# A DiT attention block: V with its features on the partitions, Wo applied before the attention weights, and the gate applied to V Wo

## The chip, the cores and the metric

The kernel runs on one core of one Trainium2 chip. A core has a matrix engine (TensorE, PE in the profile; its weight loads are listed apart as PEld), a vector engine (VectorE, DVE), an engine for activations and copies (ScalarE, ACT), a general engine (GpSimd, POOL) and a queue engine (SyncE, SP) that here only issues transfers. The engines run independently and wait for one another by semaphores. TensorE writes only to PSUM, which has 8 banks of 2 KB per partition; the other engines carry results from PSUM to SBUF, the working memory of 128 partitions. The metric is the device time of one execution in microseconds; lower is better.

## The reference

The inputs are x (2 batches of 256 tokens with 1152 features), a condition c per batch, and the weights wqkv, wo and w_mod, all in bfloat16. Cut to what matters:

```python
mod = (silu(c) @ w_mod).reshape(B, 6, 1, D)      # shift, scale, gate used
h = layernorm(x) * (1 + scale_a) + shift_a
q, k, v = split(h @ wqkv)                        # each (2, 256, 1152)
p = softmax(einsum('bqd,bkd->bqk', q, k) * D ** -0.5)
a = einsum('bqk,bkd->bqd', p, v) @ wo
return x + gate_a * a                            # one gate row per batch
```

The gate has one value for each batch and output feature; it is the same for all tokens of a batch. P V Wo can be multiplied in either order, (P V) Wo or P (V Wo), and since the gate scales output features it can be put on V Wo as well as on the result.

## The kernel before, in words

Names: P = 128 partitions, KT = 9 blocks of 128 features, TT = 4 token tiles of 128 (tiles 0 and 1 are batch 0, tiles 2 and 3 batch 1), CW = 384 columns, NCH = 3 such chunks, NQ = 2 token tiles in a batch, N = 256, T = 512 tokens.

The front of the program, up to the scores, is not touched. It loads x and the weights in one ordered list on the SP queue, normalises x, turns it so that features lie on the partitions (hT, 128 x 9 x 512), and forms K and Q with features on the partitions (qkT). The scores of a batch (s_ps) are a product of those two. The softmax goes over VectorE and ScalarE (scores, exps, probs, lines 590 to 612), and the weights P are turned by DMA (turn, line 614) into pT, with key tokens on the partitions. On the way VectorE accumulates the gate in 18 steps (gate_steps, gacc): each scales one 128-row block of the gate's weights and adds it. When they are done, two partition_all_reduce instructions on GpSimd (line 645), one for each batch, sum over partitions and leave the gate in gate_bc, in float32, the same row on every partition.

The part that the change rewrites has three stages on TensorE:

- V (v_group, line 622): for each token tile and 384-column chunk, nine matmuls with hT as the stationary operand and the V weights as the moving one, 108 in all. V comes out with tokens on the partitions; ScalarE casts each bank to v_sb (evac, first argument False).
- P V (line 663): for each batch and 128-feature block, two matmuls with v_sb stationary and pT moving, 36 in all of 256 columns. The result has features on the partitions; the casts to attnT alternate between VectorE and ScalarE.
- Wo (line 675): for each token tile, chunks of output columns of nine matmuls each, attnT stationary and wO moving. Tiles 0 to 2 have three chunks of 384, tile 3 has 448, 320, 256 and 128. VectorE multiplies each bank by the gate into ga, adds x into o_sb, and SP stores the rows. The last chunk goes another way: the 128 columns of wO for it are multiplied by the gate beforehand (gated_columns into wo_last, three times on VectorE between other work, once on GpSimd), an identity matmul brings x into the bank, and ScalarE copies it out and issues the store itself (line 711).

The order of the work is written by hand. Every instruction of TensorE, VectorE, ScalarE, SP and GpSimd is recorded through a wrapper (its line, 85, is what the profile shows for nearly all of them), and pin fixes each engine's order to that of the program text. PSUM banks are handed out in turn from a ring of eight (bank, line 66). A queue that waits for one instruction holds back everything behind it.

Of the kernel before, what the change touches and what calls it, by code (L numbers as in the profile page):

```python
# [8 lines left out]
ALU = mybir.AluOpType  # L9
AX = mybir.AxisListType  # L10
F32 = mybir.dt.float32
BF16 = mybir.dt.bfloat16
# [4 lines left out]
def kernel(  # L17
# [9 lines left out]
    nc = tc.nc  # L27
    P = 128
    B, N, D = x.shape
    T = B * N  # L30
    KT = D // P
    TT = T // P
    NQ = N // P
    CW = 384
    NCH = D // CW
# [10 lines left out]
    out_f = out.rearrange("b n d -> (b n) d")  # L46
# [7 lines left out]
    act = ctx.enter_context(tc.tile_pool(name="act", bufs=1))  # L54
    work = ctx.enter_context(tc.tile_pool(name="work", bufs=2))
    const = ctx.enter_context(tc.tile_pool(name="const", bufs=1))
# [9 lines left out]
    def bank(shape, name, dtype=None, where=None):  # L66
        if where is None:
            where = ring[turn_no[0] % len(ring)]
            turn_no[0] += 1
        return where[0].tile(shape, dtype or F32, tag=where[1], name=name)  # L70
# [21 lines left out]
    vec = _Rec(nc.vector, dve_seq)  # L92
    sca = _Rec(nc.scalar, act_seq)
    ten = _Rec(nc.tensor, pe_seq)
    spq = _Rec(nc.sync, sp_seq)
    gps = _Rec(nc.gpsimd, pool_seq)
# [13 lines left out]
    def one(t):  # L110
        return slice(t * P, (t + 1) * P)
# [3 lines left out]
    ident = const.tile([P, P], BF16)  # L115
    gps.memset(ident, 0.0)
    gps.affine_select(
        out=ident, in_=ident, compare_op=ALU.not_equal, fill=1.0, base=0,
# [8 lines left out]
        out=mask, in_=mask, compare_op=ALU.is_ge, fill=0.0, base=0,  # L127
# [3 lines left out]
        out=mask, in_=mask, compare_op=ALU.is_ge, fill=0.0, base=2,  # L131
# [4 lines left out]
    x_sb = act.tile([P, TT, D], BF16)  # L136
# [7 lines left out]
    chunks_w = [wpool.tile([P, KT, CW], BF16, tag=f"wchunk{i}", name="wV") for i in range(NCH)]  # L144
# [121 lines left out]
    hT = act.tile([P, KT, T], BF16)  # L266
# [69 lines left out]
    def evac(on_dve, out_ap, in_ap):  # L336
        if on_dve:
            return vec.tensor_copy(out=out_ap, in_=in_ap)
        return sca.copy(out=out_ap, in_=in_ap)
# [201 lines left out]
    wO = wmpool.tile([P, KT, D], BF16, tag="wH")  # L541
# [31 lines left out]
    for f in range(QACC, KT):  # L573
        ps = bank([P, T], "psQ")
# [6 lines left out]
    for b in range(B):  # L581
        s_ps = bank([P, NQ, N], "s_ps")
        for i in range(NQ):
            tq = b * NQ + i
            for k in range(KT):
                ten.matmul(s_ps[:, i, :], lhsT=qkT[:, k, tq * P : (tq + 1) * P], rhs=qkT[:, KT + k, tok(b)],
                           start=(k == 0), stop=(k == KT - 1))
        s_tiles.append(s_ps)

    nmxs, p_fs, rsums, pns, pT_sbs = {}, {}, {}, {}, []  # L590
# [26 lines left out]
            spq.dma_start_transpose(out=pT[:, :, i * P : (i + 1) * P], in_=pns[b][:, i, :])  # L617
        pT_sbs.append(pT)

    v_sb = act.tile([P, TT, D], BF16, tag="a1")  # L620

    def v_group(gidx):
        t, vc = divmod(gidx, NCH)
        wt = chunks_w[vc]
        ps = bank([P, CW], "ps")
        for k in range(KT):
            ten.matmul(ps, lhsT=hT[:, k, t * P : (t + 1) * P], rhs=wt[:, k, :], start=(k == 0), stop=(k == KT - 1))
        evac(False, v_sb[:, t, vc * CW : (vc + 1) * CW], ps)

    gate_bc = act.tile([P, B, D], F32, tag="gb")  # L630

    gate_steps(11)
# [12 lines left out]
        ar = gps.partition_all_reduce(gate_bc[:, b, :], gacc[:, b, :], P, bass.bass_isa.ReduceOp.add)  # L645
        tc.add_manual_dep(ar.ins, gate_done, SYNC_SCHED, reason="keep gpsimd off the shared port")

    for gidx in range(TT * NCH):
        v_group(gidx)

    attnT = act.tile([P, KT, T], BF16, tag="a2")
    TAIL = (128,)
    TAILW = sum(TAIL)
    wo_last = const.tile([P, KT, TAILW], BF16)

    def gated_columns(eng, k0, k1):
        eng.tensor_tensor(out=wo_last[:, k0:k1, :], in0=wO[:, k0:k1, D - TAILW :],
                          in1=gate_bc[:, B - 1, D - TAILW :].unsqueeze(1).to_broadcast([P, k1 - k0, TAILW]),
                          op=ALU.mult)

    gated_columns(gps, KT - 1, KT)

    for b in range(B):
        for gi, dv0 in enumerate(range(0, KT, 2)):
            ndv = min(2, KT - dv0)
            ps = bank([P, 2, N], "ps")
            for dd in range(ndv):
                dv = dv0 + dd
                for j in range(NQ):
                    ten.matmul(ps[:, dd, :], lhsT=v_sb[:, b * NQ + j, dv * P : (dv + 1) * P],  # L670
                               rhs=pT_sbs[b][:, j, :], start=(j == 0), stop=(j == NQ - 1))
            evac(gi % 2 == 0, attnT[:, dv0 : dv0 + ndv, b * N : (b + 1) * N], ps[:, :ndv, :])

    todo = {4: (0, 3), 6: (3, 6), 8: (6, KT - 1)}
    for t in range(TT):
        b = t // NQ
        o_sb = work.tile([P, D], BF16, tag="o_sb")
        if t < TT - 1:
            chunks = [(oc * CW, CW) for oc in range(NCH)]
            dma_after = {NCH - 1: (0, D)}  # L680
        else:
            chunks, c0 = [], 0
            for w_ in (448, 320, 256) + TAIL:
                chunks.append((c0, w_))
                c0 += w_
            dma_after = {1: (0, chunks[2][0]), 2: (chunks[2][0], D - TAILW), 3: (D - TAILW, D)}
        for ci, (c0, w_) in enumerate(chunks):
            cs = slice(c0, c0 + w_)
            last = (t == TT - 1) and (ci == len(chunks) - 1)
            pregated = (t == TT - 1) and c0 >= D - TAILW  # L690
            ps = bank([P, w_], "ps")
            if pregated:
                ten.matmul(ps, lhsT=ident, rhs=x_sb[:, t, cs], start=True, stop=False)
            for k in range(KT):
                ten.matmul(
                    ps, lhsT=attnT[:, k, t * P : (t + 1) * P],
                    rhs=(wo_last[:, k, c0 - (D - TAILW) : c0 - (D - TAILW) + w_] if pregated else wO[:, k, cs]),
                    start=(k == 0 and not pregated), stop=(k == KT - 1),
                )
            if pregated:  # L700
                sca.copy(out=o_sb[:, cs], in_=ps)
            else:
                ga = work.tile([P, 448], F32, tag="ga")
                vec.tensor_tensor(out=ga[:, :w_], in0=ps, in1=gate_bc[:, b, cs], op=ALU.mult)
                vec.tensor_tensor(out=o_sb[:, cs], in0=ga[:, :w_], in1=x_sb[:, t, cs], op=ALU.add)
                if t * NCH + ci in todo:
                    gated_columns(vec, *todo[t * NCH + ci])
            if ci in dma_after:
                d0, d1 = dma_after[ci]
                dma_eng = nc.scalar if last else spq  # L710
                dma_eng.dma_start(out=out_f[t * P : (t + 1) * P, d0:d1], in_=o_sb[:, d0:d1])

    pin(pe_seq)
    pin(dve_seq)
# [33 lines left out]
```

## Time and profile before

| | |
|---|---|
| Median of 3 runs | 95.46 us (95.27 to 95.66) |
| Profiled execution | 95.63 us, its span 93.9 us |
| PE busy | 89.2 us (95%), 664 matmuls |
| DVE busy | 69.6 us (74%) |
| ACT busy | 33.9 us (36%) |
| POOL busy | 20.8 us (22%) |
| First matmul of V | 51.67 us |
| First matmul of P V | 69.22 us |
| First matmul of Wo | 73.15 us |

The span is the time from the first to the last event that the profile of the execution shows; the execution's own time is a little longer. A line of the profile names the engine, the operation, its output and inputs as out<-in, the shapes, how often it ran, the busy time, and the idle time of its engine just ahead of it with what ended that. In the timeline the first two columns are the start and the length of a merged group, in microseconds; the last bracket is idle time and its releaser. In the windows each pair is busy time and number of pieces. The ends of matmuls are modelled, and spans on GpSimd are rough.

### The profile page before, as it was taken

The numbers are of one execution on the slowest core, as the hardware profiler recorded it, in microseconds if no ns is written. First come the engines' busy times: TensorE is split into PE (matmuls) and PEld (weight loads), VectorE is DVE, ScalarE is ACT, GpSimd is POOL, SyncE is SP. The second block draws the span as 40 slices with busy tenths as digits, with TensorE's granted clock in tenths as the row PEclk, the third lists the DMA queues.
The fourth block names the chain that finished last, engine by engine and source line by source line (L and its number), as shares of the span: only waits on it lengthen the run. The fifth ranks groups of instructions, "written<-read, shape, count | busy, mean of one in ns | idle before, by whom it ended". The sixth has DMA issues, their size and how long they took to land.

```text
span 93.9 us, 1692 instructions
## 1 busy us (share of the span) xinstructions
PE 89.2 (95%) x664; PEld 52.8 (56%) x664; DVE 69.6 (74%) x134; ACT 33.9 (36%) x69; POOL 20.8 (22%) x26
## 2 busy tenths in 40 slices
PE   3999999999999999999999999999999999999970
PEld 1348884545445444444478665656578665665660
DVE  2478789245997977999999899990028587888880
ACT  5188788002643600284220687324246200000010
POOL 5623000800000000000000000008999990002000
PEclk9999999999999999999999999999999999999999
DMA  2999999999999999999999702200000000312212
GB/s 23 345 282 374 372 397 362 369 410 407 407 405 410 414 408 412 402 373 365 381 407 410 296 17 56 63 0 0 0 0 0 0 0 8 125 42 83 114 45 92
DMA packets 17232, 21.31 MB, mean 227 GB/s; under 512 B 2249, under 2 KB 10569, under 8 KB 17225
## 3 DMA queue, kind: packets, MB, share of 16 engines
q1 hardware_dynamic: 16809, 21.17, 62.3%
q8 instruction: 5, 0.08, 0.3%
q10 hardware_dynamic: 416, 0.04, 0.3%
q14 instruction: 2, 0.02, 0.0%
HBM read 19.76 MB, written 1.18 MB: 223 GB/s over the span
## 4 chain that ended last, share of the span: by engine, by line
PE 91%; DVE 4%; issue 1%
PE ps L85 39%; PE psQ L85 19%; PE acc L85 11%; PE psK L85 7%; PE junk_ps L85 5%; PE s_ps L85 4%; PE tp L85 2%; PE psE L85 2%; PE psS L85 2%; DVE o_sb L85 2%; DVE ga L85 2%; PE psH L85 1%; DVE xc L85 1%; DVE junk L85 1%; PE bc_ps L85 0%
## 5 line engine op out<-in xcount | busy, mean ns | idle before, releaser
L85 POOL PARTITION_ALL_REDUCE gate_bc<-gacc x2 | 13.7, 6886 | 44.6 <-DVE gacc L85 44.6
L85 DVE SCALAR_TENSOR_TENSOR gacc<-wG,scT_f,gacc 128x1152 f32<-128x1152 bf16 x16 | 22.4, 1416 | 0.4
L85 PE MATMUL ps<-wV,hT 128*128 128x384 bf16 x108 | 17.7, 326 | 0.0
L85 PE MATMUL psQ<-hT,wQ 128*128 128x512 bf16 x81 | 17.6, 379 | 0.0
L85 PE MATMUL ps<-wO,attnT 128*128 128x384 bf16 (+3 forms) x108 | 17.2, 322 | 0.0
L85 PEld LDWEIGHTS <-attnT 128*128 128x128 bf16 x117 | 11.1, 98 | 6.5
L85 PEld LDWEIGHTS <-hT 128*128 128x128 bf16 x108 | 10.6, 98 | 6.9
L85 PEld LDWEIGHTS <-wK 128*128 128x128 bf16 x109 | 9.5, 97 | 6.9 <-issue 0.2
L85 PEld LDWEIGHTS <-wQ 128*128 128x128 bf16 x81 | 7.9, 98 | 9.6
L85 PE MATMUL acc<-hTs,wK 128*128 128x512 bf16 (+2 forms) x65 | 11.2, 314 | 0.0
L85 DVE TENSOR_TENSOR ga<-ps,gate_bc 128x384 f32<-128x384 f32 (+3 forms) x12 | 6.5, 545 | 3.0 <-PE ps L85 3.0
L85 ACT CAST qkT<-psQ 128x512 bf16<-128x512 f32 x9 | 4.9, 597 | 10.6 <-PE psQ L85 10.6
L85 DVE CAST attnT<-ps 128x512 bf16<-128x512 f32 (+1 forms) x6 | 3.5, 603 | 6.8 <-PE ps L85 6.8
L85 ACT CAST v_sb<-ps 128x384 bf16<-128x384 f32 x12 | 5.5, 476 | 7.9 <-PE ps L85 7.9
L85 PE MATMUL psK<-hTs,wK 128*128 128x512 bf16 x28 | 7.0, 379 | 0.0
L85 DVE TENSOR_TENSOR o_sb<-ga,x_sb 128x384 bf16<-128x384 f32 (+3 forms) x12 | 6.6, 548 | 0.4
L85 ACT CAST o_sb<-ps 128x128 bf16<-128x128 f32 x1 | 0.3, 265 | 17.3 <-PE ps L85 17.3
L85 PE MATMUL junk_ps<-junk 128*128 128x512 bf16 x11 | 4.9, 629 | 1.5 <-DVE junk L85 1.5
L85 DVE TENSOR_TENSOR hT<-hTs,held 128x512 bf16<-128x512 bf16 x9 | 5.8, 688 | 0.4 <-ACT held L85 0.4
L85 DVE BATCH_NORM_STATS2 stats<-x_sb 128x6 f32<-128x384 bf16 x6 | 3.1, 544 | 2.3 <-DMA x_sb<-in_x_dram 2.3
L85 PEld LDWEIGHTS <-junk 128*128 128x128 bf16 (+1 forms) x13 | 1.6, 134 | 5.0 <-issue 3.4
L85 PE MATMUL s_ps<-qkT 128*128 128x256 bf16 x36 | 4.1, 273 | 0.0
(81 smaller groups left out, 84.2 us busy)
## 6 DMA issues: line engine op xcount, KB each, us to landing
wG<-in_w_mod_dram SPq DMA_DIRECT2D x3, 864.0 KB, 12.5
wV<-in_wqkv_dram SPq DMA_DIRECT2D x3, 864.0 KB, 13.4
wO<-in_wo_dram SPq DMA_DIRECT2D x3, 864.0 KB, 9.0
wH<-in_w_mod_dram SPq DMA_DIRECT2D x2, 1152.0 KB, 9.3
wQ<-in_wqkv_dram SPq DMA_DIRECT2D x4, 576.0 KB, 11.7
wK<-in_wqkv_dram SPq DMA_DIRECT2D x7, 288.0 KB, 7.0
wS<-in_w_mod_dram SPq DMA_DIRECT2D x3, 320.0 KB, 6.3
x_sb<-in_x_dram SPq DMA_DIRECT2D x3, 288.0 KB, 3.4
```

What stands on the lines that cost most here:

```text
L85: r = fn(*a, **k)
```

## The change

V is formed with its features on the partitions, as Q and K already are: for each of nine feature blocks, nine matmuls with the V weights stationary and all 512 tokens moving, cast by ScalarE into vT. Then U = V Wo is formed for all tokens: vo(t, c0, w_) takes vT of one token tile as stationary and a chunk of wO as moving operand, and VectorE multiplies the bank by the batch's gate row into u_sb in bfloat16. Then attend(t, c0, w_) multiplies with P: pT stationary, u_sb moving, two matmuls for each token tile and chunk. VectorE adds x from SBUF and writes o_sb; for the last two chunks of tile 3 (on_act) an identity matmul brings x into the bank and ScalarE copies it out. The calls of vo and attend are interleaved in a written list. For batch 1 the last 384 columns are split into 256 and 128, and the last attend calls are split into a first and a last matmul step. o_sb now has all four token tiles. The columns of wO that were multiplied by the gate beforehand (wo_last, gated_columns) are gone, and so are v_sb, attnT and ga.

The stores are 288 KB each for tiles 0 and 1, then 192 KB of tile 3, 256 KB of tile 2, 64 KB of tile 3, 32 KB of tile 2, all on SP, and 32 KB of tile 3 on ScalarE's queue.

```diff
-    for gidx in range(TT * NCH):
-        v_group(gidx)
...
-    gated_columns(gps, KT - 1, KT)
...
+    vT = act.tile([P, KT, T], BF16, tag="a1")
+    for f in range(KT):
+        wt, i = chunks_w[f // NCH], f % NCH
+        ps = bank([P, T], "psV")
+        for k in range(KT):
+            ten.matmul(ps, lhsT=wt[:, k, i * P : (i + 1) * P], rhs=hT[:, k, :], start=(k == 0), stop=(k == KT - 1))
+        evac(False, vT[:, f, :], ps)
+
+    u_sb = act.tile([P, TT, D], BF16, tag="a2")
+    o_sb = act.tile([P, TT, D], BF16, name="o_sb")
+
+    def vo(t, c0, w_):
+        cs = slice(c0, c0 + w_)
+        ps = bank([P, w_], "psU")
+        for f in range(KT):
+            ten.matmul(ps, lhsT=vT[:, f, one(t)], rhs=wO[:, f, cs], start=(f == 0), stop=(f == KT - 1))
+        vec.tensor_tensor(out=u_sb[:, t, cs], in0=ps, in1=gate_bc[:, t // NQ, cs], op=ALU.mult)
+
+    def store(t, c0, c1, eng=spq):
+        eng.dma_start(out=out_f[t * P : (t + 1) * P, c0:c1], in_=o_sb[:, t, c0:c1])
+
+    pso = {}
+
+    def attend(t, c0, w_, steps=range(NQ), on_act=False):
+        b, i = divmod(t, NQ)
+        cs = slice(c0, c0 + w_)
+        for j in steps:
+            if j == 0:
+                pso[t] = bank([P, w_], "psO")
+                if on_act:
+                    ten.matmul(pso[t], lhsT=ident, rhs=x_sb[:, t, cs], start=True, stop=False)
+            ten.matmul(pso[t], lhsT=pT_sbs[b][:, j, i * P : (i + 1) * P], rhs=u_sb[:, b * NQ + j, cs],
+                       start=(j == 0 and not on_act), stop=(j == NQ - 1))
+        if NQ - 1 not in steps:
+            return
+        if on_act:
+            sca.copy(out=o_sb[:, t, cs], in_=pso[t])
+        else:
+            vec.tensor_tensor(out=o_sb[:, t, cs], in0=pso[t], in1=x_sb[:, t, cs], op=ALU.add)
+
+    CA, CB, CC = [(i * CW, CW) for i in range(NCH)]
+    CL, CE = (2 * CW, CW - P), (D - P, P)
+    vo(0, *CA)
+    vo(1, *CA)
+    vo(0, *CB)
+    attend(0, *CA)
+    vo(1, *CB)
+    attend(1, *CA)
+    vo(0, *CC)
+    attend(0, *CB)
+    vo(1, *CC)
+    attend(1, *CB)
+    vo(2, *CA)
+    attend(0, *CC)
+    store(0, 0, D)
+    vo(3, *CA)
+    attend(1, *CC)
+    store(1, 0, D)
+    vo(2, *CB)
+    attend(2, *CA)
+    vo(3, *CB)
+    attend(3, *CA)
+    vo(2, *CL)
+    attend(2, *CB)
+    vo(3, *CL)
+    attend(3, *CB)
+    store(3, 0, CL[0])
+    vo(2, *CE)
+    attend(2, *CL)
+    store(2, 0, CE[0])
+    vo(3, *CE)
+    attend(3, *CL, on_act=True)
+    store(3, CL[0], CE[0])
+    attend(2, *CE, steps=range(1))
+    attend(3, *CE, steps=range(1), on_act=True)
+    attend(2, *CE, steps=range(1, NQ))
+    attend(3, *CE, steps=range(1, NQ), on_act=True)
+    store(2, CE[0], D)
+    store(3, CE[0], D, sca)
```

More of the change, by code (lines that the diff above doesn't have):

```diff
@@ L618, in turn @@
         pT_sbs.append(pT)
[L620 to L628, printed above, removed]
     gate_bc = act.tile([P, B, D], F32, tag="gb")
@@ L646 @@
         tc.add_manual_dep(ar.ins, gate_done, SYNC_SCHED, reason="keep gpsimd off the shared port")
-    for gidx in range(TT * NCH):
-        v_group(gidx)
[L651 to L659, printed above, removed]
@@ L661 @@
-    gated_columns(gps, KT - 1, KT)
[L663 to L680, printed above, removed]
-        else:
[L682 to L711, printed above, removed]
```

## The prediction

> **What bounds the kernel now.** I read the page's busy shares and its chain first, then the windows by stage, then the timeline of the tail, and last the groups with their forms.
>
> ```profile
> PE 89.2 (95%) x664; PEld 52.8 (56%) x664; DVE 69.6 (74%) x134; ACT 33.9 (36%) x69; POOL 20.8 (22%) x26
> PEclk9999999999999999999999999999999999999999
> PE 91%; DVE 4%; issue 1%
> ```
> ```profile
> 51.67:69.22 17.55, 17.55 (x110) 10.55 (x108) 11.32 (x12) 8.80 (x23) 5.59 (x1) 1.00 0.18 57
> 69.22:73.15 3.93, 3.93 (x38) 3.52 (x36) 2.92 (x5) 2.25 (x5) 3.93 (x2) 1.00 0.00 0
> 73.15:90.22 17.07, 17.07 (x110) 10.56 (x108) 13.70 (x27) 0.57 (x1) 4.71 (x2) 1.00 0.14 53
> ```
>
> TensorE bounds it: 91% of the chain, at the full granted clock. The windows are the three stages that the change rewrites: V (51.67 to 69.22), the product with P (to 73.15), the product with Wo (to 90.22). Columns are the stretch, its length, busy time (and pieces) of PE, PEld, DVE, ACT and POOL, clock, DMA share, GB/s. In all three PE is busy for the whole stretch, so what ScalarE, VectorE and GpSimd do there is free as long as it keeps pace. Only the last microseconds are not PE's:
>
> ```profile
> 90.22 0.22 PE L85 MATMUL ps<-x_sb,ident 128*128 128x128 bf16 x1
> 90.28 0.67 PE L85 MATMUL ps<-wo_last,attnT 128*128 128x128 bf16 x9
> 90.42 0.42 DVE L85 TENSOR_TENSOR ga<-ps,gate_bc 128x256 f32<-128x256 f32 x1
> 90.49 1.18 SPq L85 DMA_DIRECT2D out_dram<-o_sb  x2
> 90.88 0.43 DVE L85 TENSOR_TENSOR o_sb<-ga,x_sb 128x256 bf16<-128x256 f32 x1
> 90.98 0.27 ACT L85 CAST o_sb<-ps 128x128 bf16<-128x128 f32 x1 [17.26 <-PE ps L85]
> 91.28 0.38 ACTq L711 DMA_DIRECT2D out_dram<-o_sb  x1
> ```
> ```profile
> out_dram<-o_sb SPq DMA_DIRECT2D x1, 64.0 KB, 1.7
> out_dram<-o_sb ACTq DMA_DIRECT2D x1, 32.0 KB, 1.6
> ```
>
> The last matmul ends at 90.95; two branches follow. ScalarE copies 128 columns and issues their store at 91.28, which lands 1.6 later, at 92.9. VectorE ends its last add at 91.31, and SP's second store (64 KB, issued at about 91.34) lands 1.7 later, at 93.04. The span ends at 93.9, 0.86 behind that. The profiled execution took 95.63 with this span, so 1.73 lies around it; the median of the runs is 95.46, 0.17 less. I work in its times and carry differences to the median.
>
> **TensorE's sum.** The price of one matmul is its start-to-start step. For 384 columns 17.55/108 = 0.1625; for 256, 3.93/36 = 0.1092; for 128, from the row at 90.28, (0.67 - 0.22)/8 = 0.056. For 512 columns a row of the chain has 19 in 4.10, 0.2158 each:
>
> ```profile
> 43.80 4.10 PE psQ L85 x19
> ```
>
> Removed: 17.55 + 3.93 + 17.07, then 0.06 for the identity matmul and 9 x 0.056 = 0.50; together 39.11, from 51.67 to 90.78. Added: V is 81 matmuls of 512 columns, 17.48. The product with Wo over all tokens is 90 of 384 (14.63), 18 of 256 (1.97) and 18 of 128 (1.01). The product with P is 20 of 384 (3.25), 5 of 256 (0.55) and 5 of 128 (0.28), counting the two identity matmuls that now bring in x. Together 39.17, to 90.84. The same columns go through the array, plus 256 more of identity: **+0.06**. The stationary operands become wV, vT and pT in place of hT, v_sb and attnT; all are 128x128 loads and already overlap today, so no price changes.
>
> **The work beside it.** Twelve ScalarE casts of V become nine of 512 columns. The ten casts of attnT, the pairs of gating and adding, three VectorE products and one GpSimd product into wo_last all go. In come 14 gating products from PSUM and 12 adds from PSUM.
>
> ```profile
> L85 ACT CAST qkT<-psQ 128x512 bf16<-128x512 f32 x9 | 4.9, 597 | 10.6 <-PE psQ L85 10.6
> L85 DVE TENSOR_TENSOR ga<-ps,gate_bc 128x384 f32<-128x384 f32 x9 | 5.0, 556 | 2.8 <-PE ps L85 2.8
> L85 DVE TENSOR_TENSOR o_sb<-ga,x_sb 128x384 bf16<-128x384 f32 x9 | 5.0, 559 | 0.3
> ```
>
> VectorE: 10 x 0.556 + 2 x 0.425 + 2 x 0.29 for the gates and 10 x 0.559 + 0.425 + 0.29 for the adds, 13.3 in the 20.2 between 70.6 and 90.8. It is no bound. Removing its former work gains nothing: that work lay beside a PE that never waited for it. The same holds for GpSimd's single product, and for ScalarE's casts of V: each 512-column cast is 0.6 against 9 x 0.2158 = 1.94 of matmuls. If that cover were gone they would cost their own time, but only the last cast is near the path: V ends at 69.15, its last sum is in PSUM at about 69.31, the cast ends near 69.95, and the ninth matmul of the first Wo chunk, the first to read it, comes at 69.15 + 8 x 0.1625 = 70.45. Slack 0.5.
>
> A gate must be done before the product with P that reads it. In the list each attend stands at least one Wo chunk (1.46, or 0.98 and 0.50 in the tail) behind the Wo chunk whose gate it needs, and a gate needs about 0.6. The wait is added to PE's queue, with all later matmuls behind it; on this working it is already met, save at two places.
>
> **First place: the gate rows themselves.** Today nothing needs gate_bc before 74.89; now the first gate could start at 70.8.
>
> ```profile
> 63.63 13.69 POOL L85 PARTITION_ALL_REDUCE gate_bc<-gacc  x2 [44.62 <-DVE gacc L85]
> 74.89 0.56 DVE L85 TENSOR_TENSOR ga<-ps,gate_bc 128x384 f32<-128x384 f32 x1 [1.11 <-PE ps L85]
> 81.26 0.56 DVE L85 TENSOR_TENSOR o_sb<-ga,x_sb 128x384 bf16<-128x384 f32 x1
> 81.73 0.55 DVE L85 TENSOR_TENSOR wo_last<-wO,gate_bc 128x384 bf16<-128x384 bf16 x1
> L85 POOL PARTITION_ALL_REDUCE gate_bc<-gacc x2: 6851/6886/6921, 63.6 to 70.4; - x2
> ```
>
> By these rows the first reduction ends at 70.5, but the profile calls GpSimd's spans rough, and all that is sure is that the first half was there by 74.89 and the second by 81.73. PE comes to the first attend at 69.15 + 3 x 1.4625 = 73.54 and needs two gates done: a start, a second start 0.47 behind it (the step from 81.26 to 81.73), its 0.56, and the hop to PE, some 1.1 in all. So the reduction may end as late as 72.4 without cost; past that every microsecond costs one, up to 74.89 + 1.1 - 73.54 = 2.45. I take the row (70.5): cost 0, with 0 and 2.45 as ends. The second half is read by the attend at 84.27, so it may come as late as 83.1, and it came by 81.73: cost 0.
>
> **Second place: the tail.** Walking back from 90.84, the 256-column Wo chunk of token tile 3 ends its issue at 88.68. Behind it in PE's order stand 0.325 (attend, 384), 0.504 (Wo, tile 2, 128), 0.218 (attend, 256), 0.504 (Wo, tile 3, 128), 0.328 (attend with identity, 256) and then 0.056 + 0.112 of first steps and 2 x 0.056 of last steps. The last steps need the gate of the last Wo chunk. Two latencies come from rows: PSUM to VectorE, the 128-column sum is 0.16 behind its issue step and the engine starts 0.04 later; VectorE to PE 0.06 (8.38 to 8.44):
>
> ```profile
> 7.87 0.51 DVE L85 TENSOR_SCALAR xc<-x_sb,nmean 128x1152 bf16<-128x1152 bf16 x1
> 8.44 0.34 PE L85 MATMUL tp<-ident,xc 128*128 128x128 bf16 x3 [0.23 <-DVE xc L85]
> ```
>
> VectorE gates at 88.88, adds at 89.22, gates 128 columns at 89.71, adds 256 at 89.93 (end 90.36). The last Wo chunk ends its issue at 90.23, so the last gate runs from 90.43 to 90.72, and PE may go on at 90.78; it arrives at 90.73. Wait 0.05. No row has this operation at 128 columns from float32 PSUM: 0.425 at 256 and 0.556 at 384 give 0.29 by the same slope; 0.28 (a 128-column tensor_scalar from PSUM) and 0.425 are its ends:
>
> ```profile
> L85 DVE TENSOR_TENSOR ga<-ps,gate_bc 128x256 f32<-128x256 f32 x1 | 0.4, 425 | 0.0
> L85 DVE TENSOR_SCALAR hTs<-tp,s1p 128x128 bf16<-128x128 bf16 x4 | 1.0, 279 | 0.5 <-PE tp L85 0.5
> ```
>
> If in addition the independent VectorE operations don't overlap (0.56 and 0.43 apart, not 0.47 and 0.34), the last gate ends between 91.0 and 91.25 and PE waits 0.3 to 0.6. I take 0.05, since the step of 0.47 is in the trace.
>
> Then the last sum is there at 91.06, ScalarE copies until about 91.36 and issues at 91.39 (0.11 later than today). SP has six stores in place of five, the last ones 256 KB at about 90.4, 64 KB at 91.15 (behind ScalarE's 256-column copy) and, as one issue holds SP for 0.33, the last 32 KB at 91.48. At 1.6 that lands at 93.08, 0.04 past today's 93.04. The 256 KB have a microsecond before them, so I charge nothing for sharing.
>
> **Sum.** +0.06 on PE, +0.05 of waiting, of which today's longer VectorE branch absorbs most: +0.04 to +0.11 at the end, so a span of 93.95 to 94.0, 95.7 beside the profiled 95.63, and 95.53 beside the median. I call **95.5**.
>
> **The rivals.** (a) *The gate comes late* and PE stands still once, at the first attend. For it: the roughness of GpSimd's rows, and that nothing needed the tile so early. Against it: two equal rows of 6.9, the second starting where the first ends. It decides from 72.9 on; at 74.0 it gives 97.1, at most 97.9. This is slower than before. (b) *VectorE falls behind in the tail*: PE waits 0.3 to 0.6, giving 95.8 to 96.1. Against it: VectorE is 66% busy in the stage. (c) *Weight loads set the step of narrow matmuls.* There are now 23 of 128 columns where there were ten; at the load's own length of 0.098 instead of 0.056 they cost 23 x 0.042 = 0.97, so 96.4.
>
> ```profile
> 90.22 0.55 PEld L85 LDWEIGHTS <-attnT 128*128 128x128 bf16 x9
> L85 PEld LDWEIGHTS <-attnT 128*128 128x128 bf16 x117 | 11.1, 98 | 6.5
> ```
>
> Nine such loads started within 0.55 - 0.10, 0.056 apart, and kept PE's step; I give this 3 in 100. [...] (d) *Faster*: PE's sum can't shrink, and without any wait the last store would land 0.1 sooner. Half a microsecond would have to come from the unchanged first 51.67, whose scatter shows in the runs (95.27 to 95.66).
>
> **Chances.** Half a per cent (0.48) is about what a measurement of this kernel can tell from no change. Forecast 0.64; (a) 0.12, of it 0.03 still within half a per cent; (b) 0.10, about all of it counted as over that bound once small misses elsewhere add to it; (c) 0.03; unpriced slower 0.04; (d) 0.07. So faster 0.07, same 0.67, slower 0.26. The forecast's own range is 95.2 to 95.85. To leave out no more than 2 in 10 the range goes down to 95.1 and up to 96.6, through (b), (c) and the cheaper half of (a).
>
> **What would show it.** V's 81 matmuls in 17.5; PE without a gap from 51.67 to about 90.7; the first gate at 70.8 and the first attend at 73.5; the reductions unchanged; ScalarE's last store at 91.4. A first gate near 73 or later proves (a); idle PE before the last two matmuls of 0.3 proves (b); Wo chunks of 128 columns that take 0.9 prove (c). The prediction is wrong if PE has holes between Wo chunks and attends that this list doesn't show, or if the time before 51.67 moves.

## The result and the profile after

The changed kernel takes 104.81 us (median of 6 runs, 104.55 to 105.8) beside 95.53 for the kernel before in the same comparison; the ratio is 1.0977, with a 95% interval of 1.0943 to 1.101. It is 9.3 us slower, where 95.5 was forecast. One execution further down, 108.05 us of the kernel with more filler matmuls, lay more than 1.5% above the fastest of its kernel and is left out of its ratio.

The profiled execution is the slowest of the six: 105.8, with a span of 103.9, 10.0 longer than the span before; so its rows have 10.0 to account for, where the medians differ by 9.3. Its page, with the busy shares, the clock and the chain:

```profile
PE 91.4 (88%) x639; PEld 51.8 (50%) x639; DVE 64.3 (62%) x127; ACT 31.7 (30%) x63; POOL 20.4 (20%) x25
PE   4940049999999999999999999999999999999980
PEclk9998555699999999999999999999999999999999
PE 83%; issue 9%; POOL 3%; DVE 1%; ACT 1%; POOLq 0%
```

Each digit of the slices is 2.6 us. TensorE is idle in slices 4 and 5, its granted clock falls to five tenths in slices 5 to 7, and the chain has 9% of "issue", time in which an engine waited for nothing that the profile shows. All of this lies ahead of the code that the diff touches. The windows, with columns as in the prediction, set the rewritten part apart:

```profile
0.00:10.00 10.00, 4.82 (x11) 1.58 (x12) 1.50 (x3) 4.01 (x6) 0.39 (x5) 0.98 0.81 257
10.00:20.00 10.00, 5.68 (x59) 5.05 (x59) 5.26 (x17) 2.80 (x5) 4.00 (x11) 0.51 1.09 382
20.00:61.49 41.49, 41.49 (x334) 22.95 (x333) 34.02 (x70) 15.46 (x30) 2.31 (x7) 1.00 0.88 324
61.49:103.90 42.41, 39.37 (x239) 22.23 (x236) 23.55 (x38) 9.42 (x23) 13.69 (x2) 1.00 0.11 35
```

V starts at 61.49 in place of 51.67, 9.82 later. From there to the end it takes 42.41, where the kernel before took 93.9 - 51.67 = 42.23. So the rewritten stages cost 0.18, and the 9.8 were lost in code that is the same in both kernels. GpSimd's timeline of the changed kernel says where:

```profile
0.78 0.20 POOL L85 MEMSET ident<- 128x128 bf16 x1 [0.29 <-POOLq L739]
10.21 0.28 POOL L85 TENSOR_SCALAR_AFFINE_SELECT ident<-ident 128x128 bf16<-128x128 bf16 x1 [9.22 <-issue]
...
12.38 0.14 POOL L85 MEMSET ones_row<- 1x64 bf16 x1
12.61 0.32 POOL L85 TENSOR_SCALAR e_sb<-e_sb 128x18 f32<-128x18 f32 x1
...
73.45 13.69 POOL L85 PARTITION_ALL_REDUCE gate_bc<-gacc  x2 [44.62 <-DVE gacc L85]
```

And of the kernel before, the same instruction at the start and the last one of GpSimd:

```profile
1.28 0.29 POOL L85 TENSOR_SCALAR_AFFINE_SELECT ident<-ident 128x128 bf16<-128x128 bf16 x1 [0.29 <-POOL ident L85]
...
84.95 0.54 POOL L85 TENSOR_TENSOR wo_last<-wO,gate_bc 128x128 bf16<-128x128 bf16 x1 [7.63 <-issue]
```

GpSimd's first affine_select, which builds the identity matrix, starts 8.93 later, behind a gap of 9.22 that nothing in the profile ends. Everything at the start waits behind it in GpSimd's queue: the row of ones for TensorE (12.38, before 3.45), the "+1" of the silu (12.61, before 4.19), and with them the scales. The kernel before has a gap of the same kind, 7.63 long, but ahead of its product into wo_last, beside a busy TensorE. That product is what the change removes.

The order of GpSimd's instructions in the two built programs lists an ISA instruction at those places. Before, from the end of the front on:

```
24 L85 TensorCopy parts_sq<-rest 128x4
25 L85 ISA
26 L85 ISA gate_bc<-gacc 128x1152 x2
27 L85 ISA
28 L85 TensorTensor wo_last<-wO,gate_bc 128x128
```

The changed program ends with row 26. Both have such a row between the first memset and the first affine_select. The traces record it under the name MODIFY_POOL_CONFIG: at 1.00 in the changed kernel, and at 1.18 and 77.27 in the kernel before. Its own record is 0.09 us long at most; the gap, where there is one, lies between it and the next instruction. Row 25 comes at 18.96, just ahead of the 44.62 for which GpSimd waits for the gate, so a gap behind it would not show.

### The profile page after: what moved, and what is told of

It is laid out like the page before. It is cut to its first block, busy times and chain, and to the rows that moved or that the text cites. A ratio compares the mean times of both kernels' runs of the same rounds, so it can differ in the third digit from the quotient of the medians.

```text
span 103.9 us, 1622 instructions
## 1 busy us (share of the span) xinstructions
PE 91.4 (88%) x639; PEld 51.8 (50%) x639; DVE 64.3 (62%) x127; ACT 31.7 (30%) x63; POOL 20.4 (20%) x25
## 3 DMA queue, kind: packets, MB, share of 16 engines
HBM read 19.76 MB, written 1.18 MB: 202 GB/s over the span
## 4 chain that ended last, share of the span: by engine, by line
PE 83%; issue 9%; POOL 3%; DVE 1%; ACT 1%; POOLq 0%
PE psU L85 17%; PE psV L85 17%; PE psQ L85 17%; PE acc L85 10%; PE psK L85 6%; PE s_ps L85 4%; PE psO L85 4%; PE tp L85 4%; PE psS L85 2%; PE psE L85 2%; POOL mask L85 2%; PE psH L85 1%; ACT o_sb L85 1%; DVE xc L85 1%; POOL ident L85 0%
## 5 line engine op out<-in xcount | busy, mean ns | idle before, releaser
L85 PE MATMUL psU<-wO,vT 128*128 128x384 bf16 (+2 forms) x126 | 19.6, 303 | 0.0
L85 PE MATMUL psV<-hT,wV 128*128 128x512 bf16 x81 | 17.6, 379 | 0.0
L85 DVE TENSOR_TENSOR u_sb<-psU,gate_bc 128x384 bf16<-128x384 f32 (+2 forms) x14 | 7.0, 500 | 15.4 <-PE psU L85 15.3
L85 PEld LDWEIGHTS <-vT 128*128 128x128 bf16 x126 | 11.7, 98 | 6.5
L85 PEld LDWEIGHTS <-wV 128*128 128x128 bf16 x81 | 7.9, 98 | 9.4
L85 ACT CAST vT<-psV 128x512 bf16<-128x512 f32 x9 | 5.1, 582 | 8.3 <-PE psV L85 8.1
L85 PEld LDWEIGHTS <-xc 128*128 128x128 bf16 x36 | 3.3, 133 | 8.2 <-DVE xc L85 8.2
L85 DVE TENSOR_TENSOR o_sb<-psO,x_sb 128x384 bf16<-128x384 f32 (+2 forms) x12 | 6.2, 516 | 0.3 <-PE psO L85 0.3
L85 PE MATMUL psO<-u_sb,pT 128*128 128x384 bf16 (+2 forms) x28 | 6.0, 303 | 0.0
L85 PE MATMUL tp<-ident,xc 128*128 128x128 bf16 x36 | 4.1, 289 | 1.8 <-DVE xc L85 1.8
```

The source lines that it names most:

```text
L85: r = fn(*a, **k)
```

## The experiments

**Theory A**: the gap comes ahead of GpSimd's first ordinary operation (an affine_select or a product) behind a partition_all_reduce, in the same execution or, where the reduction comes last, at the start of the next. In the kernel before, the product behind the reductions took it beside TensorE (7.63); without that product it stands ahead of the next execution's first affine_select (9.22). The expectations below call the gap a fetch of code; that is the author's conjecture, which no trace here shows, and the runs test only where the gap stands. **Rivals**: (B) the new buffers, layout or matrix stages delay the start; (C) any GpSimd work behind the reductions would do, of whatever kind; (D) the loss belongs to the reordered products.

**One small product behind the reductions.**

```diff
         tc.add_manual_dep(ar.ins, gate_done, SYNC_SCHED, reason="keep gpsimd off the shared port")
+    closing = const.tile([P, TT], F32)
+    gps.tensor_tensor(out=closing, in0=neg_half, in1=neg_half, op=ALU.mult)
```

> The changed kernel with one 128x4 product on GpSimd behind the two reductions. Theory A (the gap of 9.22 us ahead of GpSimd's first affine_select is GpSimd fetching the code for its ordinary operations, because the execution before ended with the reduction's code in place): the product takes that gap behind the reductions, some 7.6 us beside TensorE, the gap at the start shrinks to 0.29 as in the kernel before, and the time is 95.5 to 96.0. Rival B (the gap comes from the new buffers or the new layout of SBUF, or from the rewritten matrix stages): the gap and the time stay, 104.5 to 105.8.

Measured: 96.17 beside 95.81 for the kernel before on that chip, ratio 1.0032 (1.0005 to 1.0059); that is a little above the 95.5 to 96.0 expected. The gap moved back, as two rows of this kernel's GpSimd timeline show:

```profile
1.28 0.29 POOL L85 TENSOR_SCALAR_AFFINE_SELECT ident<-ident 128x128 bf16<-128x128 bf16 x1 [0.29 <-POOL ident L85]
...
85.27 0.19 POOL L85 TENSOR_TENSOR closing<-neg_half 128x4 f32<-128x4 f32 x1 [7.61 <-issue]
```

An instruction of 0.19 us, whose result nobody reads, takes 9 us off the time: the ratio goes from 1.0977 to 1.0032, and 0.0945 of 95.8 is 9.05. The layout, but for one small tile, and the matrix stages are those of the changed kernel, so B and D fall.

**A memset in its place.**

```diff
+    closing = const.tile([P, TT], F32)
+    gps.memset(closing, 0.0)
```

> The same, with a 128x4 memset in place of the product; memsets ran at 0.78 us in the changed kernel, ahead of the gap. Theory A: a memset fetches nothing, so the gap of some 9 us at the start stays and the time is 104.5 to 105.8. Rival C (any work of GpSimd behind the reductions, or a longer GpSimd program, takes the gap away): 95.5 to 96.0.

Measured: 106.19 in one run, 0.4 above the range expected for theory A and 10 away from C. The built program has no MODIFY_POOL_CONFIG between the reductions and the memset, and the gap stays at the start:

```profile
11.06 0.28 POOL L85 TENSOR_SCALAR_AFFINE_SELECT ident<-ident 128x128 bf16<-128x128 bf16 x1 [10.06 <-issue]
...
87.37 0.17 POOL L85 MEMSET closing<- 128x4 f32 x1
```

The memset starts at 87.37, where the rough span of the reductions ends at 73.81 + 13.69 = 87.50; so it follows them at once. So C falls: not work, but the kind of work, moves the gap.

**The kernel before without its GpSimd product.** VectorE does those columns too.

```diff
-    gated_columns(gps, KT - 1, KT)
-    todo = {4: (0, 3), 6: (3, 6), 8: (6, KT - 1)}
+    todo = {4: (0, 3), 6: (3, 6), 8: (6, KT)}
```

> The kernel before, with its single GpSimd product into wo_last moved to VectorE (the third of the three VectorE products grows from 256 to 384 columns, 0.13 us more beside TensorE). Theory A: the gap appears at the start of this kernel too, 104.3 to 105.8. Rivals B and D (the loss belongs to the reordered products with Wo and P): 95.3 to 95.8.

Measured: 104.79, ratio 1.0939 (1.0896 to 1.0982). Taking one instruction of 0.54 us off GpSimd in the old kernel gives the loss again, within the two intervals, with no reordering at all:

```profile
10.01 0.28 POOL L85 TENSOR_SCALAR_AFFINE_SELECT ident<-ident 128x128 bf16<-128x128 bf16 x1 [9.02 <-issue]
```

**No reductions at all.** GpSimd copies the partial sums of each partition. The kernel leaves out the sum over partitions, so its gate is not that of the reference.

```diff
-        ar = gps.partition_all_reduce(gate_bc[:, b, :], gacc[:, b, :], P, bass.bass_isa.ReduceOp.add)
+        ar = gps.tensor_copy(out=gate_bc[:, b, :], in_=gacc[:, b, :])
```

> The changed kernel without the two reductions: GpSimd copies each partition's own partial sums into gate_bc, so the gate is wrong and the sum over partitions is left out. No other code is fetched in the program, so theory A expects the affine_select at 1.3 us, no gap behind the copies, and 95.3 to 96.3. A rival by which the start suffers from the new layout or the new matrix stages expects the gap and 104 or more.

Measured: 96.3 in one run. The affine_select starts at 1.07, and the copies follow VectorE's last gate step without a gap of their own:

```profile
1.07 0.29 POOL L85 TENSOR_SCALAR_AFFINE_SELECT ident<-ident 128x128 bf16<-128x128 bf16 x1
...
63.88 2.23 POOL L85 COPY gate_bc<-gacc 128x1152 f32<-128x1152 f32 x2 [44.54 <-DVE gacc L85]
```

With no reduction the changed kernel has no such gap anywhere: in these runs the gap appears only in programs with both kinds of work.

**Why 9 at the start and 7.6 behind the reductions.** SP's first load was put behind the first affine_select, so that the loads of x and the weights do not run during the gap.

```diff
+    first_select = pool_seq[-1].ins.name
...
     load_x(0)
+    tc.add_manual_dep(sp_seq[0].ins, first_select, SYNC_SCHED, reason="loads behind the first select")
```

> The changed kernel with SP's first load behind GpSimd's first affine_select, so that no weights or x move while GpSimd waits. If the gap at the start (9.0 to 10.1 us) is longer than the one behind the reductions (7.6) because it shares the DMA engines with the loads, it shrinks to 7.3 to 8.0; if it is longer for another reason, it stays at 9 or more. The time itself is longer by some microseconds in either case, 106 to 112.

Measured: 105.78 in one run, under the 106 expected. The gap shrank to 7.30:

```profile
8.29 0.28 POOL L85 TENSOR_SCALAR_AFFINE_SELECT ident<-ident 128x128 bf16<-128x128 bf16 x1 [7.30 <-issue]
```

The windows of the gap in the changed kernel, in this one, and behind the reductions in the kernel before (the two last columns are the share of the DMA engines and GB/s):

```profile
1.00:10.00 9.00, 4.82 (x11) 1.58 (x12) 1.47 (x3) 3.80 (x6) 0.00 (x0) 0.98 0.90 286
1.00:8.28 7.28, 4.87 (x11) 1.58 (x12) 0.45 (x1) 1.28 (x2) 0.00 (x0) 1.00 0.02 1
77.40:84.90 7.50, 7.50 (x48) 4.53 (x47) 6.15 (x13) 0.00 (x0) 0.00 (x0) 1.00 0.20 78
```

So the gap is 9.02 to 10.06 in four profiles beside the loads, which in the changed kernel keep the DMA engines busy for 0.90 of it; it is 7.30 where their share is 0.02, and behind the reductions 7.63 in the kernel before, at a share of 0.20, and 7.61 and 7.25 in the two kernels with the closing product: what GpSimd waits for seems to share something with the loads. Which resource that is, no run here shows. The time came out no worse, although the first load starts at 8.60 in place of 0.79: the gap is 1.92 shorter, and from the affine_select to the first reduction it takes 65.09 in place of 63.24, which gives 1.85 back.

What GpSimd does in the gap, no trace here shows. In the gap of the changed kernel no packet runs on the two DMA queues of the kind "instruction", and their packets and bytes are the same in that kernel as in the one without reductions (5 and 2 packets, 0.08 and 0.02 MB). The runs show when the gap comes and goes.

**Is the clock a part of the loss?** In the changed kernel TensorE idles from 6.3 to 12.6, and the granted clock is 0.51 between 10 and 20.

```diff
-    fillers(11)
+    fillers(38)
```

> The changed kernel with 38 in place of 11 filler matmuls at the start, so that TensorE stays busy over the gap. If the idle stretch from 6.3 to 12.6 us costs a slower granted clock on top of the wait (0.51 in the stretch from 10 to 20), the time falls by 0.3 to 1.2 us, to 103.6 to 104.5; if the wait alone costs, it stays at 104.8 within 0.3.

Measured: ratio 1.0943 (1.0912 to 1.0974), where the changed kernel has 1.0977 (1.0943 to 1.101). The times do not settle it: 0.3 us lower, with overlapping intervals, where 0.3 to 1.2 was expected. In the profiles, from the affine_select to the first reduction, the kernel before takes 63.63 - 1.28 = 62.35, the changed one 73.45 - 10.21 = 63.24, and this one 72.79 - 10.34 = 62.45. Its window over the start and its GpSimd row:

```profile
10.00:20.00 10.00, 6.84 (x73) 5.63 (x71) 5.18 (x16) 3.01 (x6) 4.01 (x11) 0.83 1.09 381
...
10.34 0.28 POOL L85 TENSOR_SCALAR_AFFINE_SELECT ident<-ident 128x128 bf16<-128x128 bf16 x1 [9.35 <-issue]
...
72.79 13.69 POOL L85 PARTITION_ALL_REDUCE gate_bc<-gacc  x2 [44.61 <-DVE gacc L85]
```

With the filler matmuls the clock of that stretch is 0.83 in place of 0.51, and this profile is 0.79 shorter there than the changed kernel's. But the same distance is 62.75 and 62.80 in the two other profiles of a gap beside the loads (with the memset, and the kernel before without its product), and it scatters from 62.35 to 62.81 in the four profiles without a gap at the start (62.69 with the closing product, 62.64 with the shorter tail). Nor do the executions tell: of the changed kernel's six, two have a mean granted clock of 1.0, with spans of 102.8 and 103.1, beside 102.7 to 103.9 for the four at 0.95 to 0.97. So a cost of the slower clock is not shown. The 10.0 of the profiled execution are 8.93 of gap, 0.89 between there and the reductions, of which the clock may be a part, and 0.18 of tail.

**A shorter tail.** With the closing product, the 256-column chunk of tile 3 was moved from the identity matmul and ScalarE to VectorE, and two stores of tile 3 became one.

```diff
-    attend(3, *CL, on_act=True)
-    store(3, CL[0], CE[0])
+    attend(3, *CL)
...
-    store(3, CE[0], D, sca)
+    store(3, CL[0], D, sca)
```

> The changed kernel with the GpSimd product behind the reductions, and a shorter tail: the 256-column chunk of tile 3 gets x on VectorE and not by an identity matmul and ScalarE, and the last 384 columns of tile 3 leave in one store on ScalarE's queue, so that SP has five stores in place of six. If the sixth store waits for SP's issue slot and PE's 256 identity columns count (0.11), the end comes 0.2 to 0.35 us sooner than with the product alone: ratio to the kernel before 0.998 to 1.001. If the end is set by the last matmul and ScalarE's copy alone, 0.1 us sooner: 1.002.

Measured: 95.85 beside 95.87, ratio 0.9993 (0.9973 to 1.0014). The last stores on SP, of the kernel with the closing product and of this one:

```profile
91.91 0.41 SPq L85 DMA_DIRECT2D out_dram<-o_sb  x1
```
```profile
91.62 0.33 SPq L85 DMA_DIRECT2D out_dram<-o_sb  x1
```

SP's last issue comes 0.29 sooner, and the ratio lies in the range expected, 0.998 to 1.001. Against the closing product alone that is 0.4% less, though the two intervals still touch. By this ratio the shorter tail makes up for what the rewritten tail cost, and no version that was run is shown to be faster than the kernel before.

## Why the prediction was wrong

**The step that failed** is in "The work beside it": "Removing its former work gains nothing", and "The same holds for GpSimd's single product". The product's 0.54 us were indeed free, so nothing was gained; but the sum put at nothing, without a reason, what its removal could cost. The product was the last ordinary operation of GpSimd, and it held the 7.63 that stood before it, as "issue" idle time in GpSimd's timeline of the kernel before, in a stretch where TensorE covered it. Remove it, and 9 us come back where nothing covers them. The run that takes out that product alone (ratio 1.0939) and the run that puts an ordinary operation back (1.0032) show it from both sides. The change was priced by what each removed instruction costs; an unexplained 7.6 in front of one of them went unasked. Of the prediction's chances only the 0.04 for "unpriced slower" covers this outcome, and nothing there gives it a size.

**The rival for a gain** said that half a microsecond "would have to come from the unchanged first 51.67", and the prediction named a move of that time as a way to be wrong. It was the right place and the wrong size and sign: code that isn't in the diff ran 9.8 later.

**The sum for the rewritten stages holds.** From V's first matmul the profile after gives, by the prediction's terms:

```profile
61.39 17.26 PEld L85 LDWEIGHTS <-wV 128*128 128x128 bf16 x81
61.49 17.65 PE L85 MATMUL psV<-hT,wV 128*128 128x512 bf16 x81
80.71 0.56 DVE L85 TENSOR_TENSOR u_sb<-psU,gate_bc 128x384 bf16<-128x384 f32 x1 [7.49 <-PE psU L85]
...
99.54 0.67 PE L85 MATMUL psU<-wO,vT 128*128 128x128 bf16 x9
100.24 0.29 DVE L85 TENSOR_TENSOR u_sb<-psU,gate_bc 128x128 bf16<-128x128 f32 x1
100.48 0.38 PE L85 MATMUL psO<-u_sb,pT 128*128 128x128 bf16 x3
101.19 0.36 ACTq L85 DMA_DIRECT2D out_dram<-o_sb  x1
```

- TensorE ends 100.86 - 61.49 = 39.37 behind V's start, before 90.95 - 51.67 = 39.28: +0.09, where the sum gave +0.06 and a wait of 0.05.
- ScalarE's store is issued at 39.70 of that clock, before at 39.61: +0.09, where 0.11 was worked out.
- The end is +0.18 in this profile, and 94.4 - 52.01 - 42.23 = +0.16 with the closing product, where +0.04 to +0.11 was worked out. The term that was too small is the end of SP's queue: its sixth store is issued at 91.91 - 52.01 = 39.90 behind V's start, worked out as 91.48 - 51.67 = 39.81.
- The 128-column gate from PSUM, interpolated as 0.29, is 0.29.

**The rivals.** (a) is refuted: the first gate starts at 80.71 - 61.49 = 19.22 behind V's start (70.8 - 51.67 = 19.13 was expected), where PSUM released it and not the reduction. So the first reduction was over 80.71 - 73.45 = 7.26 behind its start at the latest, which fits its row of 6.9. (b) did not happen: the profile shows no idle time of TensorE in the tail, and TensorE ends only 0.09 later behind V's start than before. (c) is refuted: nine matmuls of 128 columns have a step of (0.67 - 0.22)/8 = 0.056 with vT stationary too, and V's 81 matmuls of 512 columns have a step of (17.65 - 0.38)/80 = 0.216.

With the closing product the ratio is 1.0032 (1.0005 to 1.0059), and the forecast, 95.53 beside 95.46, is 1.0007. So the forecast describes that version; it does not describe the kernel that was changed.

## What to carry to other kernels

Before an instruction is removed because its own time is hidden, ask what it leaves behind for the next instruction of its engine, and for the next execution: an idle gap that the profile puts down to "issue" ahead of it is a cost that may turn up in another place, as the 7.63 ahead of the product here turned up as 9.22 at the start. Where a kernel uses partition_all_reduce and ordinary GpSimd operations, try a tiny ordinary operation at the end of GpSimd's program, at a time when GpSimd is idle anyway; here it took the ratio from 1.0977 to 1.0032. And when an unchanged stretch of code moves, compare its first late instruction with what the program last did on that engine.

## What the runs showed of the hardware

- Behind the reductions GpSimd stands idle for 7.25 to 7.63 us ahead of a tensor_tensor (7.63 in the kernel before, with the DMA engines busy for 0.20 of the time). At the start of the kernels whose program ends with a reduction, or with a memset behind it, it stands idle ahead of the affine_select for 9.02 to 10.06 beside the loads (a share of 0.90 in the changed kernel), and for 7.30 with the loads held back (0.02). The memset behind the reductions starts at 87.37, where their rough span ends at 87.50: it has no gap.
- Each of the five kernels whose GpSimd program ends with a reduction, or with a memset behind it, has the gap at the start of its profiled execution; the three that end with an ordinary operation behind the reductions, and the one with no reduction, don't. The reading that an execution finds what the one before it left rests on this pattern. The record does not say what ran directly ahead of each execution, so that part is inferred.
- In the profiled execution of the changed kernel TensorE idles for 6.24 us at the start and its granted clock is 0.51 from 10 to 20; with fillers, which shorten the idle time to 1.38, it is 0.83. What the slower clock costs is not shown.
